# One decode-attention kernel on one core: values loaded two units at a time, keys of two units ahead of the values of both

## The chip, the cores and the metric

The kernel runs on one core of one Trainium2 chip. The metric is device time in microseconds (us) of one execution. The core has a matrix engine (TensorE, PE in the profile, with its weight loads shown apart as PEld), a vector engine (VectorE, DVE), a scalar engine (ScalarE, ACT), a general engine (GpSimd, POOL) and a sync engine (SyncE, SP) that here does nothing but issue DMA transfers and wait. Data comes from the off-chip memory (HBM) through 16 DMA engines into SBUF; TensorE writes to PSUM, and VectorE and ScalarE copy from there.

## The reference

One query token, 32 query heads, 8 key/value heads, 65,536 keys, head size 128, all bf16. Each key/value head serves R = 4 query heads.

```python
B, Hq, Hkv, Sq, Sk, D = 1, 32, 8, 1, 65536, 128
scale = D ** -0.5
scores = jnp.einsum("bhqd,bhkd->bhqk", q, k) * scale
p = _softmax(scores, axis=-1)
return jnp.einsum("bhqk,bhkd->bhqd", p, v)
```

Keys and values are 134.2 MB each, and each byte is used once, for four queries. Nothing of the result needs them twice.

## The kernel before

**Units.** A head's 65,536 keys are cut into HU = 4 units of 16,384 keys; with 8 heads there are NU = 32 units, numbered through. A unit of keys is one transfer of 4,096 KB: 128 partitions, each with a row of 32 KB that is contiguous in HBM (128 keys of 256 bytes). The same holds for a unit of values. There are two buffers for keys (`kbuf`) and two for values (`vbuf`); unit n uses number n % 2 of both.

**Keys of a unit** (`pe_keys`, L156). Keys lie with the key index on partitions, and a product over the head size needs them turned, so TensorE transposes them: 16 groups of TB = 8 transposes (L138) into one of four PSUM buffers (`trb`). Each group is copied to SBUF (`ktb`, `evict`, L220): groups 3, 7, 11 and 15 by ScalarE (L228), the other twelve by VectorE (L230). LAG = 3 groups later, eight matmuls (L149) with the copied keys as weights and the four queries as the moving operand write the scores (`qkb`, two buffers). A unit is done with its key buffer when its last group has been transposed, and `evict` then raises `kfree`.

**Softmax of a unit.** It is the running form: VectorE reduces the maximum per partition (L261), GpSimd takes it over all partitions (L384), VectorE makes the new maximum and its negative (L276 to L278), ScalarE makes the correction factor `alpha` and four exponentials with their sums (L350, L354) into `pts`. VectorE then rescales the running output `acc` and the running sum `lp` (L289 to L291).

**Values of a unit** (`pe_values`, L171). 128 matmuls (L168) add up the unit's output in PSUM. They wait for the load (`vrdy`) and for the exponentials (`exd`). VectorE adds the result to `acc` (`add_values`, L243) and raises `vfree`, which gives the value buffer back.

**Order on TensorE** (L211). A loop of 16 rounds, in each: keys of an even unit, values of the odd unit before it, keys of the odd unit, values of the even unit. So a unit's softmax runs while the next unit's keys are on TensorE. After the loop, `pe_last` (L178) does the values of unit 31.

**Order on VectorE and ScalarE.** VectorE's pass for unit u (`dve_pass`, L254) mixes the end of unit u with the evictions of unit u + 1: score maximum of u, output of u - 1, evictions 0 to 2 of u + 1, new maximum, six more evictions, sums and rescaling, the last three evictions. ScalarE does the same with its four evictions and the exponentials (`act_pass`, L344).

**Order of the loads.** SP issues all loads on one queue in the order K0, K1, V0, K2, V1, K3, V2, ..., K31, V30, V31. Each key load waits for `kfree` (L403), each value load for `vfree` (L413). The first and the last unit of keys come in two halves. The last unit of values comes in six pieces of 64, 32, 16, 10, 4 and 2 of the 128 rows' parts (`V_PIECES`), and `pe_last` waits for each piece, so that little is left to do when the last piece lands: 126 matmuls in the usual form, two in another form (L197), one that adds the running output (L201), a scaling (L339) and the store of the last head.

Of the kernel before, what the change touches and what calls it, by code (L numbers as in the profile page):

```python
# [5 lines left out]
DT = mybir.dt  # L6
# [4 lines left out]
P = 128  # L11
# [32 lines left out]
def bass_standalone__gqa_softmax__decode_kernel(nc, q, k, v, out):  # L44
# [6 lines left out]
    scale = float(D) ** -0.5  # L51
    kf, vf, qf, of = k[0], v[0], q[0, :, 0, :], out[0, :, 0, :]
# [28 lines left out]
    alpha = sb("alpha", [P, R], DT.float32)  # L81
# [19 lines left out]
    vrdy = [sem(f"vrdy{i}") for i in range(2)]  # L101
    vpiece = [sem(f"vpiece{i}") for i in range(len(V_PIECES))]
    kfree = [sem(f"kfree{i}") for i in range(2)]
    vfree = [sem(f"vfree{i}") for i in range(2)]
# [10 lines left out]
    def has_k(u):  # L115
        return u + 1 < NU

    def passes(e, one, start, period, last):

        for u in range(-1, start):  # L120
            one(u)
        n = (NU - 2 - start) // period
        with e.Fori(0, n):
            for u in range(start, start + period):
                one(u)
        for u in range(start + n * period, last + 1):
            one(u)
# [38 lines left out]
    def value(pe, b, t, first, last):  # L166
        vv = vbuf[b][:, :].rearrange("p (t d) -> p t d", d=D)
        return pe.matmul(pvb[b][:, 0:R], lhsT=vv[:, t, :], rhs=pts[b][:, t * R:(t + 1) * R],  # L168
                         start=t == first, stop=t == last)

    def pe_values(pe, b):  # L171
        take(pe, vrdy[b], 16)
        take(pe, exd)
        for t in range(T):
            ins = value(pe, b, t, 0, T - 1)
        ins.then_inc(pvd, 1)

    def pe_last(pe):  # L178
        b = (NU - 1) % 2
        vv = vbuf[b][:, :].rearrange("p (t d) -> p t d", d=D)  # L180
        starts = [sum(V_PIECES[:i]) for i in range(len(V_PIECES))]
        pe.wait_ge(t_o, 1)
        pe.transpose(qkb[0][0:HR - R, 0:P], oT[:, R:HR], identf[:, :]).then_inc(s_o, 1)
        take(pe, exd)
        for t in range(ROWS_FROM):
            if t == starts[1]:
                pe.wait_ge(t_lp, 1)
                pe.matmul(fin[0:R, P:P + 1], lhsT=lp[:, :], rhs=ones[:, :],
                          start=True, stop=True).then_inc(s_l, 1)
            if t == starts[-2]:  # L190
                pe.wait_ge(t_last, 1)
            ins = value(pe, b, t, 0, ROWS_FROM - 1)
            if t in starts:
                ins.wait_op(vpiece[starts.index(t)], 16, "sem-ge")
        ins.then_inc(pvd, 1)
        for t in range(ROWS_FROM, T):
            ins = pe.matmul(fin[0:R, 0:P], lhsT=pts[b][:, t * R:(t + 1) * R], rhs=vv[:, t, :],  # L197
                            start=t == ROWS_FROM, stop=False)
            if t in starts:
                ins.wait_op(vpiece[starts.index(t)], 16, "sem-ge")  # L200
        ins = pe.matmul(fin[0:R, 0:P], lhsT=acc[:, :], rhs=identf[:, :], start=False, stop=True)  # L201
        ins.wait_op(t_acc, 1, "sem-ge")
        ins.then_inc(s_fin, 1)

    def tensor_engine(pe):
        pe.wait_ge(q_sem, 16)
        pe.wait_ge(t_id, 1)
        pe.transpose(trb[0][:, 0:HR], qsb[:, :], ident[0:HR, 0:HR]).then_inc(s_x, 1)  # L208
        pe.wait_ge(t_qT, 1)
        pe.addr_align(256, offset=LOOP_SLOT, max_nops=16)  # L210
        with pe.Fori(0, NU // 2) as i:  # L211
            pe_keys(pe, 0)
            with pe.If(i > 0):
                pe_values(pe, 1)
            pe_keys(pe, 1)
            pe_values(pe, 0)
        pe_last(pe)
# [25 lines left out]
    def add_values(e, w):  # L243
        take(e, pvd)
        e.sem_inc(vfree[w % 2], 1)  # L245
        pv = pvb[w % 2][:, 0:R]
        if w % HU == 0:
            own(e, e.tensor_copy(acc[:, :], pv), xd)  # L248
        else:
            own(e, e.tensor_tensor(acc[:, :], acc[:, :], pv, ALU.add), xd)  # L250
        if w % HU == HU - 1:
            own(e, e.tensor_tensor(oT[:, HR - R:HR], acc[:, :], recip[:, :], ALU.mult), xd)

    def dve_pass(e, u):  # L254
        if u >= 0:
            take(e, qkd)
            if u % HU == HU - 1 and has_k(u):
                next_queries(e, qrdy)
            elif has_k(u):
                e.sem_inc(qrdy, 1)  # L260
            e.tensor_reduce(cmax[:, :], qkb[u % 2][:, :].rearrange("p (t g) -> p g t", g=R),  # L261
                            AX.X, ALU.max).then_inc(cm, 1)
        if u >= 1 and has_k(u):
            add_values(e, u - 1)
        part = [[j for j in range(a, b) if not on_act(j)] for a, b in ((0, 4), (4, 12), (12, G))]
        if has_k(u):
            for j in part[0]:
                evict(e, u + 1, j)
        if u >= 0:
            take(e, cma)  # L270
            mn, mo = m[u % 2], m[(u - 1) % 2]
            if u % HU == 0:
                e.tensor_copy(mn[:, :], cmaxa[:, :])
                e.tensor_scalar(negm[:, :], cmaxa[:, :], -scale, None, ALU.mult).then_inc(ng, 1)
            else:
                own(e, e.tensor_tensor(mn[:, :], mo[:, :], cmaxa[:, :], ALU.max), xd)  # L276
                e.tensor_tensor(dm[:, :], mo[:, :], mn[:, :], ALU.subtract)  # L277
                e.tensor_scalar(negm[:, :], mn[:, :], -scale, None, ALU.mult).then_inc(ng, 1)  # L278
        if has_k(u):
            for j in part[1]:  # L280
                evict(e, u + 1, j)
        if not has_k(u):
            add_values(e, u - 1)
        if u >= 0:
            take(e, sx)
            if u % HU == 0:
                own(e, e.tensor_copy(lp[:, :], rsum[:, :]), xd)
            else:
                own(e, e.tensor_tensor(acc[:, :], acc[:, :], alpha[:, :], ALU.mult), xd)  # L289
                own(e, e.tensor_tensor(lp[:, :], lp[:, :], alpha[:, :], ALU.mult), xd)  # L290
                own(e, e.tensor_tensor(lp[:, :], lp[:, :], rsum[:, :], ALU.add), xd)  # L291
            if u % HU == HU - 1 and has_k(u):
                e.sem_inc(lrd, 1)
        if has_k(u):
            for j in part[2]:
                evict(e, u + 1, j)
        if u >= 0 and u % HU == HU - 1 and has_k(u):
            take(e, lra)
            own(e, e.reciprocal(recip[:, :], la[:, :]), xd)
            own(e, e.tensor_copy(otmp[:, 0:HR - R], oT[:, R:HR]), xd)  # L300
            own(e, e.tensor_copy(oT[:, 0:HR - R], otmp[:, 0:HR - R]), xd)
# [15 lines left out]
    def vector_engine(e):  # L317
# [7 lines left out]
        passes(e, lambda u: dve_pass(e, u), 1, HU, NU - 4)  # L325
        e.sem_inc(t_o, 1)
        for u in range(NU - 3, NU):
            dve_pass(e, u)
# [15 lines left out]
    def act_pass(e, u):  # L344
        if has_k(u):
            evict(e, u + 1, 3)
        if u >= 0:
            take(e, ng)
            if u % HU:
                e.activation(alpha[:, :], dm[:, :], AF.Exp, scale=scale)  # L350
            sv = qkb[u % 2][:, :].rearrange("p (t g) -> p g t", g=R)
            pv = pts[u % 2][:, :].rearrange("p (t g) -> p g t", g=R)
            for g in range(R):
                ins = e.activation(pv[:, g, :], sv[:, g, :], AF.Exp, bias=negm[:, g:g + 1],  # L354
                                   scale=scale, accum_out=rsum[:, g:g + 1])
            own(e, ins, xa)
            e.sem_inc(exd, 1)
            e.sem_inc(sx, 1)
        if has_k(u):
            for j in (7, 11, 15):  # L360
                evict(e, u + 1, j)

    def scalar_engine(e):
# [3 lines left out]
        passes(e, lambda u: act_pass(e, u), 0, HU, NU - 1)  # L367
# [21 lines left out]
    def src(x, n):  # L389
        h, c = n // HU, n % HU  # L390
        return x[h, c * P * T:(c + 1) * P * T, :].rearrange("(p t) d -> p (t d)", p=P)

    def sync_engine(e):
# [16 lines left out]
        def load_v(n):  # L410
            b = n % 2
            if n >= 2:
                e.wait_ge(vfree[b], n // 2)  # L413
            if n == NU - 1:
                pieces(vbuf[b], src(vf, n), V_PIECES, vpiece)
            else:
                e.dma_start(vbuf[b][:, :], src(vf, n)).then_inc(vrdy[b], 16)
# [45 lines left out]
```

## Time and profile before

| What | Value |
|---|---|
| Median of 3 runs | 631.81 us (631.73 to 631.89) |
| The profiled execution's own time | 631.78 us |
| Its span, first to last instruction | 629.9 us |
| Bytes read from HBM | 268.44 MB |
| TensorE busy | 517.2 us, 82% |
| VectorE busy | 312.8 us, 50% |
| ScalarE busy | 182.4 us, 29% |
| Mean granted TensorE clock | 0.772 |

The span is the time between the first and the last instruction that the profile shows; 1.9 us of the execution lie outside of it. A row of a timeline has the start in us from the span's start, the length in us, the engine and line, the operation, what it writes and reads, how many instructions were merged, and in brackets how long the engine stood idle before and what ended that. "SPq" and the like are the engine's sequencer, which waits and issues. In a windows table each engine has its busy time and its number of instructions, followed by the granted TensorE clock (1.00 is full), the busy share of the DMA engines and the rate.

### The profile page before, as it was taken

The page shows a single profiled execution, that of the slowest core. Times are in us where ns is not written, and L with a number is a line of the kernel's source. Part 1 is how long each engine was busy: PE and PEld are TensorE (multiplying, and loading weights), DVE is VectorE, ACT ScalarE, POOL GpSimd, SP SyncE. Part 2 cuts the span into 40 slices and gives each one's busy share as a digit, 9 for nine tenths or more (in the row PEclk, how much of TensorE's full clock was granted, in tenths as well). Part 3 has the DMA queues.
Part 4 walks back from the last instruction along what each step waited for, and adds up shares of the span by engine and source line. Part 5 has one row for each costly group of instructions (what it writes and reads, how often), then busy time and mean ns, then how long its engine had stood idle before and what let it go on. Part 6 is the DMA issues. An engine that isn't in the chain of part 4 may idle for free. (4 is left out here: it accounts for less than half of the span.)

```text
span 629.9 us, 26837 instructions
## 1 busy us (share of the span) xinstructions
PE 517.2 (82%) x12294; PEld 509.2 (81%) x12294; DVE 312.8 (50%) x689; ACT 182.4 (29%) x410; POOL 15.9 (3%) x49
## 2 busy tenths in 40 slices
PE   4678987789788798877888788987879787798897
PEld 4678987789788788877888778987879787788896
DVE  5435654446544455534565344653446544455552
ACT  2213332133322233221332213332223322233231
POOL 0000000000000000000000000000000000000000
PEclk9788876788767787767877678876778776787776
DMA  8999999999999999999999999999999999999996
GB/s 366 431 430 433 431 433 433 431 433 433 431 433 433 433 433 431 431 429 431 431 433 433 433 433 433 431 429 433 431 429 431 431 433 433 433 433 433 421 442 285
DMA packets 10335, 268.61 MB, mean 426 GB/s; under 512 B 1235, under 2 KB 1491, under 8 KB 1747
## 3 DMA queue, kind: packets, MB, share of 16 engines
q1 hardware_dynamic: 10232, 268.44, 99.3%
q8 instruction: 7, 0.11, 0.1%
q14 instruction: 6, 0.04, 0.0%
q10 hardware_dynamic: 90, 0.02, 0.0%
HBM read 268.44 MB, written 0.01 MB: 426 GB/s over the span
## 5 line engine op out<-in xcount | busy, mean ns | idle before, releaser
L138 PE MATMUL trb<-ident,kbuf 128*128 128x128 bf16 x4096 | 354.7, 245 | 76.9 <-PEq L41 76.9
L138 PEld LDWEIGHTS trb<-ident,kbuf 128*128 128x128 bf16 x4096 | 287.9, 111 | 78.7 <-issue 78.6
L230 DVE COPY ktb<-trb 128x1024 bf16<-128x1024 bf16 x384 | 255.7, 690 | 157.4 <-PE trb L138 152.3
L228 ACT ACTIVATE ktb<-trb 128x1024 bf16<-128x1024 bf16 x128 | 131.0, 1023 | 435.2 <-PE trb L138 376.2
L149 PE MATMUL qkb<-qcur,ktb 128*128 128x4 bf16 x4096 | 172.5, 165 | 23.5 <-PEq L41 20.7
L149 PEld LDWEIGHTS qkb<-qcur,ktb 128*128 128x128 bf16 x4096 | 155.5, 97 | 27.0 <-issue 25.1
L168 PE MATMUL pvb<-pts,vbuf 128*128 128x4 bf16 x4094 | 112.3, 165 | 5.2 <-issue 2.0
L168 PEld LDWEIGHTS pvb<-pts,vbuf 128*128 128x128 bf16 x4094 | 110.2, 101 | 7.2 <-issue 4.6
L354 ACT ACTIVATE pts<-qkb,negm 128x128 bf16<-128x128 f32 x128 | 50.8, 551 | 0.0
L261 DVE TENSOR_REDUCE cmax<-qkb 128x4 f32<-128x512 f32 x32 | 22.1, 692 | 38.6 <-DVEq L41 37.6
L354 ACT ACTIVATION_READ_ACCUMULATOR pts<-qkb,negm 128x1 f32 x128 | 36.1, 282 | 0.0
L250 DVE TENSOR_TENSOR acc<-acc,pvb 128x4 f32<-128x4 f32 x23 | 3.6, 159 | 60.3 <-DVEq L41 60.3
L384 POOL PARTITION_ALL_REDUCE cmaxa<-cmax x32 | 11.8, 370 | 503.4 <-POOLq L41 503.4
L248 DVE COPY acc<-pvb 128x4 f32<-128x4 f32 x8 | 1.3, 161 | 24.2 <-DVEq L41 24.2
L239 DVE COPY qcur<-qT 128x4 bf16<-128x4 bf16 x8 | 1.4, 170 | 11.6 <-DVEq L41 11.5
L291 DVE TENSOR_TENSOR lp<-lp,rsum 128x4 f32<-128x4 f32 x24 | 3.9, 163 | 3.5
L277 DVE TENSOR_TENSOR dm<-m 128x4 f32<-128x4 f32 x24 | 3.9, 162 | 3.5
L290 DVE TENSOR_TENSOR lp<-lp,alpha 128x4 f32<-128x4 f32 x24 | 3.9, 162 | 3.5
L350 ACT ACTIVATE alpha<-dm 128x4 f32<-128x4 f32 x24 | 4.7, 198 | 2.7 <-ACTq L41 2.7
L387 POOL PARTITION_ALL_REDUCE la<-lp x7 | 3.0, 429 | 99.1 <-POOLq L41 99.1
L208 PE MATMUL trb<-ident,qsb 32*128 32x32 bf16 x1 | 0.2, 204 | 5.1 <-DMA qsb<-in_q_dram 5.1
L208 PEld LDWEIGHTS trb<-ident,qsb 32*128 32x128 bf16 x1 | 0.1, 100 | 5.1 <-DMA qsb<-in_q_dram 5.1
(43 smaller groups left out, 31.0 us busy)
## 6 DMA issues: line engine op xcount, KB each, us to landing
vbuf<-in_v_dram SPq DMA_DIRECT2D x31, 4096.0 KB, 31.4
kbuf<-in_k_dram SPq DMA_DIRECT2D x30, 4096.0 KB, 26.9
kbuf<-in_k_dram SPq DMA_DIRECT2D x4, 2048.0 KB, 16.7
vbuf<-in_v_dram SPq DMA_DIRECT2D x1, 2048.0 KB, 17.1
vbuf<-in_v_dram SPq DMA_DIRECT2D x1, 1024.0 KB, 19.3
vbuf<-in_v_dram SPq DMA_DIRECT2D x1, 512.0 KB, 20.1
vbuf<-in_v_dram SPq DMA_DIRECT2D x1, 320.0 KB, 20.4
vbuf<-in_v_dram SPq DMA_DIRECT2D x1, 128.0 KB, 20.2
```

What stands on the lines that cost most here:

```text
L138: ins = pe.transpose(trb[j % NTB][:, i * P:(i + 1) * P], kv[:, t, :], ident[:, :])
L149: ins = pe.matmul(qkb[b][:, t * R:(t + 1) * R], lhsT=ktb[:, off:off + P], rhs=qcur[:, :], start=True, stop=True)
L168: return pe.matmul(pvb[b][:, 0:R], lhsT=vv[:, t, :], rhs=pts[b][:, t * R:(t + 1) * R], start=t == first, stop=t == last)
L228: ins = e.activation(dst, trb[j % NTB][:, :], AF.Copy).then_inc(eva, 1)
L230: ins = e.tensor_copy(dst, trb[j % NTB][:, :]).then_inc(evd, 1)
L261: e.tensor_reduce(cmax[:, :], qkb[u % 2][:, :].rearrange("p (t g) -> p g t", g=R), AX.X, ALU.max).then_inc(cm, 1)
L277: e.tensor_tensor(dm[:, :], mo[:, :], mn[:, :], ALU.subtract)
L290: own(e, e.tensor_tensor(lp[:, :], lp[:, :], alpha[:, :], ALU.mult), xd)
L291: own(e, e.tensor_tensor(lp[:, :], lp[:, :], rsum[:, :], ALU.add), xd)
L350: e.activation(alpha[:, :], dm[:, :], AF.Exp, scale=scale)
L354: ins = e.activation(pv[:, g, :], sv[:, g, :], AF.Exp, bias=negm[:, g:g + 1], scale=scale, accum_out=rsum[:, g:g + 1])
L384: e.partition_all_reduce(cmaxa[:, :], cmax[:, :], P, bass.bass_isa.ReduceOp.max).then_inc(cma, 1)
```

## The change

Two things are put in pairs. The two value buffers become one of twice the size, which takes the values of two units in one load with rows of 64 KB; one semaphore `vrdy` tells of its landing and one `vfree` of its release, after the values of both units. And the work is ordered in rounds of two units a and b: TensorE does keys a, keys b, values a, values b.

So that the pair is contiguous in HBM, `src` cuts a head into two blocks of 32,768 keys, and each partition owns 64 KB of a block in place of 32 KB. A key load still brings 4,096 KB into one of two buffers: it takes the first or the second 32 KB of each partition's 64 KB. Which keys form a unit changes, the result does not. The queue's order becomes K0, K1, V0+1, K2, K3, V2+3, ..., K30, K31, V30, and the six pieces of V31; the value load of a round waits for `vfree` of the round before.

VectorE's and ScalarE's passes are written as rounds of two units with the same instructions. In VectorE's, the evictions of unit a stand alone, those of unit b are mixed with the softmax of a, and the softmax of b and the outputs of a and b follow them. `alpha` gets two buffers. The rescaling of `acc` moves to just ahead of the addition, and the last head's part of `oT` moves to `next_output`.

```diff
-    vbuf = [sb(f"vbuf{i}", [P, T * D], DT.bfloat16) for i in range(2)]
+    vbuf = sb("vbuf", [P, 2 * T * D], DT.bfloat16)
...
     def pe_values(pe, b):
-        take(pe, vrdy[b], 16)
+        if b == 0:
+            take(pe, vrdy, 16)
         take(pe, exd)
...
-        with pe.Fori(0, NU // 2) as i:
+        with pe.Fori(0, NR) as i:
             pe_keys(pe, 0)
-            with pe.If(i > 0):
-                pe_values(pe, 1)
             pe_keys(pe, 1)
             pe_values(pe, 0)
+            with pe.If(i < NR - 1):
+                pe_values(pe, 1)
         pe_last(pe)
...
+    def dve_round(e, i):
+        a, b = 2 * i, 2 * i + 1
+        evictions(e, a, PART)
+        scores_done(e, a)
+        evictions(e, b, PART[:1])
+        maximum(e, a)
+        evictions(e, b, PART[1:2])
+        add_sums(e, a)
+        evictions(e, b, PART[2:])
+        scores_done(e, b)
+        maximum(e, b)
+        add_sums(e, b)
+        rescale(e, a)
+        add_values(e, a)
+        rescale(e, b)
+        if i < NR - 1:
+            add_values(e, b)
+            e.sem_inc(vfree, 1)
+            if b % HU == HU - 1:
+                next_output(e)
...
+    def act_round(e, i):
+        a, b = 2 * i, 2 * i + 1
+        for j in (3, 7, 11, 15):
+            evict(e, a, j)
+        evict(e, b, 3)
+        exponentials(e, a)
+        for j in (7, 11, 15):
+            evict(e, b, j)
+        exponentials(e, b)
...
-    def src(x, n):
-        h, c = n // HU, n % HU
-        return x[h, c * P * T:(c + 1) * P * T, :].rearrange("(p t) d -> p (t d)", p=P)
+    def src(x, u, units=1):
+
+        h, c, half = u // HU, u % HU // 2, u % 2
+        rows = x[h, c * 2 * P * T:(c + 1) * 2 * P * T, :].rearrange("(p t) d -> p (t d)", p=P)
+        return rows[:, half * T * D:(half + units) * T * D]
...
-        load_k(0)
-        for n in range(NU - 1):
-            load_k(n + 1)
-            load_v(n)
-        load_v(NU - 1)
+        for i in range(NR):
+            load_k(2 * i)
+            load_k(2 * i + 1)
+            if i:
+                e.wait_ge(vfree, i)
+            if i < NR - 1:
+                e.dma_start(vbuf[:, :], src(vf, 2 * i, 2)).then_inc(vrdy, 16)
+        e.dma_start(vbuf[:, 0:T * D], src(vf, NU - 2)).then_inc(vrdy, 16)
+        pieces(vbuf[:, T * D:2 * T * D], src(vf, NU - 1), V_PIECES, vpiece)
```

NR is NU // 2 = 16 rounds. `scores_done`, `maximum`, `add_sums`, `rescale`, `add_values` and `exponentials` hold the instructions that `dve_pass` and `act_pass` had for one unit.

More of the change, by code (lines that the diff above doesn't have):

```diff
@@ L116, in has_k, with rounds @@
         return u + 1 < NU
[L118 to L127, printed above, removed]
+    def rounds(e, one):
+        with e.Fori(0, H - 1):
+            for i in range(HALVES):
+                one(i)
+        return range(NR - HALVES, NR)
     def pe_transposes(pe, b, j):
@@ L241, in next_queries, with evictions, scores_done, maximum @@
         own(e, e.tensor_copy(qT[:, 0:HR - R], qtmp[:, 0:HR - R]), xd)
-    def add_values(e, w):
+    PART = [[j for j in range(a, b) if not on_act(j)] for a, b in ((0, 4), (4, 12), (12, G))]
+    def evictions(e, n, parts):
+        for part in parts:
+            for j in part:
+                evict(e, n, j)
+    def scores_done(e, u):
+        take(e, qkd)
+        if u % HU == HU - 1 and has_k(u):
+            next_queries(e, qrdy)
+        elif has_k(u):
+            e.sem_inc(qrdy, 1)
+        e.tensor_reduce(cmax[:, :], qkb[u % 2][:, :].rearrange("p (t g) -> p g t", g=R),
+                        AX.X, ALU.max).then_inc(cm, 1)
+    def maximum(e, u):
+        take(e, cma)
+        mn, mo = m[u % 2], m[(u - 1) % 2]
+        if u % HU == 0:
+            e.tensor_copy(mn[:, :], cmaxa[:, :])
+            e.tensor_scalar(negm[:, :], cmaxa[:, :], -scale, None, ALU.mult).then_inc(ng, 1)
+        else:
+            own(e, e.tensor_tensor(mn[:, :], mo[:, :], cmaxa[:, :], ALU.max), xd)
+            e.tensor_tensor(dm[:, :], mo[:, :], mn[:, :], ALU.subtract)
+            e.tensor_scalar(negm[:, :], mn[:, :], -scale, None, ALU.mult).then_inc(ng, 1)
+    def add_sums(e, u):
+        take(e, sx)
+        if u % HU == 0:
+            own(e, e.tensor_copy(lp[:, :], rsum[:, :]), xd)
+        else:
+            own(e, e.tensor_tensor(lp[:, :], lp[:, :], alpha[u % 2][:, :], ALU.mult), xd)
+            own(e, e.tensor_tensor(lp[:, :], lp[:, :], rsum[:, :], ALU.add), xd)
+        if u % HU == HU - 1 and has_k(u):
+            e.sem_inc(lrd, 1)
+    def rescale(e, u):
+        if u % HU:
+            own(e, e.tensor_tensor(acc[:, :], acc[:, :], alpha[u % 2][:, :], ALU.mult), xd)
+    def add_values(e, u):
         take(e, pvd)
-        e.sem_inc(vfree[w % 2], 1)
-        pv = pvb[w % 2][:, 0:R]
-        if w % HU == 0:
+        pv = pvb[u % 2][:, 0:R]
+        if u % HU == 0:
             own(e, e.tensor_copy(acc[:, :], pv), xd)
@@ L250, in add_values @@
             own(e, e.tensor_tensor(acc[:, :], acc[:, :], pv, ALU.add), xd)
[L251 to L301, printed above, removed]
@@ L303, in identities, with next_output @@
+    def next_output(e):
+        take(e, lra)
+        own(e, e.reciprocal(recip[:, :], la[:, :]), xd)
+        own(e, e.tensor_copy(otmp[:, 0:HR - R], oT[:, R:HR]), xd)
+        own(e, e.tensor_copy(oT[:, 0:HR - R], otmp[:, 0:HR - R]), xd)
+        own(e, e.tensor_tensor(oT[:, HR - R:HR], acc[:, :], recip[:, :], ALU.mult), xd)
     def identities(e):
@@ L324, in vector_engine @@
         e.sem_inc(qrdy, 1)
-        passes(e, lambda u: dve_pass(e, u), 1, HU, NU - 4)
+        rest = rounds(e, lambda i: dve_round(e, i))
         e.sem_inc(t_o, 1)
-        for u in range(NU - 3, NU):
-            dve_pass(e, u)
+        for i in rest:
+            dve_round(e, i)
         e.sem_inc(t_lp, 1)
@@ L341, in vector_engine, with exponentials @@
         ins.then_inc(t_last, 1)
[L344 to L361, printed above, removed]
+    def exponentials(e, u):
+        take(e, ng)
+        if u % HU:
+            e.activation(alpha[u % 2][:, :], dm[:, :], AF.Exp, scale=scale)
+        sv = qkb[u % 2][:, :].rearrange("p (t g) -> p g t", g=R)
+        pv = pts[u % 2][:, :].rearrange("p (t g) -> p g t", g=R)
+        for g in range(R):
+            ins = e.activation(pv[:, g, :], sv[:, g, :], AF.Exp, bias=negm[:, g:g + 1],
+                               scale=scale, accum_out=rsum[:, g:g + 1])
+        own(e, ins, xa)
+        e.sem_inc(exd, 1)
+        e.sem_inc(sx, 1)
+    def act_round(e, i):
[7 more added lines that the diff above has]
+        exponentials(e, b)
     def scalar_engine(e):
@@ L366, in scalar_engine @@
         e.activation(dscr[:, 1:2], dscr[:, 0:1], AF.Exp, scale=1.0)
-        passes(e, lambda u: act_pass(e, u), 0, HU, NU - 1)
+        for i in rounds(e, lambda i: act_round(e, i)):
+            act_round(e, i)
         e.wait_ge(t_row, 1)
```

23 lines of the change are left out of this document (8 added, 15 removed).

## The prediction, made before the change was run

> **What bounds the kernel now.** I read the page first, for the engine that is never idle.
>
> ```profile
> span 629.9 us, 26837 instructions
> ...
> PE 517.2 (82%) x12294; PEld 509.2 (81%) x12294; DVE 312.8 (50%) x689; ACT 182.4 (29%) x410; POOL 15.9 (3%) x49
> ...
> DMA  8999999999999999999999999999999999999996
> GB/s 366 431 430 433 431 433 433 431 433 433 431 433 433 433 433 431 431 429 431 431 433 433 433 433 433 431 429 433 431 429 431 431 433 433 433 433 433 421 442 285
> ...
> q1 hardware_dynamic: 10232, 268.44, 99.3%
> ```
>
> The reader is to see that the DMA engines are busy in every slice but the first and the last, 99.3% of the span on the load queue, at one steady rate, while TensorE has 18% to spare. The loads bound the kernel. What can move the time is the rate of the loads, a hole in their queue, or what is left after the last load.
>
> Next the waits of SP and the page's list of issues, to see how full the queue stands.
>
> ```profile
> SPq L407 <- ACTq L226: 403.8, 29, 18.0
> SPq L417 <- DVEq L245: 142.5, 29, 7.0
> ```
>
> ```profile
> vbuf<-in_v_dram SPq DMA_DIRECT2D x31, 4096.0 KB, 31.4
> kbuf<-in_k_dram SPq DMA_DIRECT2D x30, 4096.0 KB, 26.9
> ```
>
> SP waits nearly always for a buffer, yet a load lands only 26.9 to 31.4 us after its issue. The timeline gives the time of one 4,096 KB load. TensorE starts on the keys of units 29, 30 and 31 here, the first two on their landing, and in 29 to 30 one load of keys and one of values pass.
>
> ```profile
> 568.47 3.57 PE L138 MATMUL trb<-ident,kbuf 128*128 128x128 bf16 x32 [2.35 <-PEq L41]
> 587.90 3.57 PE L138 MATMUL trb<-ident,kbuf 128*128 128x128 bf16 x32 [2.14 <-PEq L41]
> 600.60 0.34 PE L149 MATMUL qkb<-qcur,ktb 128*128 128x4 bf16 x8 [0.66 <-PEq L41]
> 601.05 3.52 PE L168 MATMUL pvb<-pts,vbuf 128*128 128x4 bf16 x128
> 604.43 3.57 PE L138 MATMUL trb<-ident,kbuf 128*128 128x128 bf16 x32
> 604.81 0.16 DVE L250 TENSOR_TENSOR acc<-acc,pvb 128x4 f32<-128x4 f32 x1 [2.93 <-DVEq L41]
> 608.87 0.61 PE L138 MATMUL trb<-ident,kbuf 128*128 128x128 bf16 x8
> 609.31 0.34 PE L149 MATMUL qkb<-qcur,ktb 128*128 128x4 bf16 x8
> 609.51 0.61 PE L138 MATMUL trb<-ident,kbuf 128*128 128x128 bf16 x8
> 617.30 0.34 PE L149 MATMUL qkb<-qcur,ktb 128*128 128x4 bf16 x8 [0.67 <-PEq L41]
> 617.63 3.49 PE L168 MATMUL pvb<-pts,vbuf 128*128 128x4 bf16 x128
> 617.79 0.69 DVE L261 TENSOR_REDUCE cmax<-qkb 128x4 f32<-128x512 f32 x1 [1.64 <-DVEq L41]
> 618.69 0.37 POOL L384 PARTITION_ALL_REDUCE cmaxa<-cmax  x1 [16.24 <-POOLq L41]
> 621.28 0.28 ACT L354 ACTIVATION_READ_ACCUMULATOR pts<-qkb,negm 128x1 f32 x1
> 621.93 1.87 PE L168 MATMUL pvb<-pts,vbuf 128*128 128x4 bf16 x64 [0.57 <-DMA vbuf<-in_v_dram]
> 626.51 0.56 PE L168 MATMUL pvb<-pts,vbuf 128*128 128x4 bf16 x14 [0.22 <-DMA vbuf<-in_v_dram]
> 627.00 0.37 PE L197 MATMUL pvb<-vbuf,pts 128*4 128x128 bf16 x2
> 627.94 0.34 DVE L339 TENSOR_SCALAR olast<-pvb,rl 4x128 bf16<-4x128 f32 x1 [0.68 <-PE pvb L201]
> ```
>
> 587.90 - 568.47 = 19.43 us for two loads, so one **slot** of 4,096 KB is 9.71 us. This stretch is also the kernel's end: the last scores are done at 617.30 + 0.34 = 617.64, the exponentials of unit 31 at 621.28 + 0.28 = 621.56, and from 621.93 on TensorE waits for each piece of the last values. The last load of values before the pieces, and nothing of TensorE, sets the time. The chain of waits agrees:
>
> ```profile
> 606.07 20.40 DMA vbuf<-in_v_dram
> 626.46 0.05 issue
> 626.51 0.56 PE pvb L168 x14
> ```
>
> So the last loads end at 626.46, and 627.07 - 626.46 = 0.6 us later the 126 matmuls are done.
>
> **The change, part by part.** First the steady rounds. Let L be the landing of a value pair. The next two key units land at L + 9.71 and L + 19.43, the next pair at L + 38.86 (four slots). TensorE does two units of values in 3.52 + 3.49 = 7.0 us, starts on keys a at about L + 10.3 (0.6 us behind a landing, as at the end above), and needs for one unit of keys:
>
> ```profile
> 296.47 3.57 PE L138 MATMUL trb<-ident,kbuf 128*128 128x128 bf16 x32 [2.75 <-PEq L41]
> 309.62 0.34 PE L149 MATMUL qkb<-qcur,ktb 128*128 128x4 bf16 x8 [0.66 <-PEq L41]
> 319.52 1.01 PE L138 MATMUL trb<-ident,kbuf 128*128 128x128 bf16 x8
> 320.59 1.01 PE L138 MATMUL trb<-ident,kbuf 128*128 128x128 bf16 x8
> ```
>
> That is 309.96 - 296.47 = 13.5 us here, 600.94 - 587.90 = 13.0 and 617.64 - 604.43 = 13.2 above; I take **13.2**. Every unit here starts slow and then speeds up, and the windows table shows why:
>
> ```profile
> 604.40:608.00 3.60, 3.60 (x45) 3.60 (x42) 2.30 (x5) 0.00 (x0) 0.00 (x0) 0.50 1.09 469
> 608.90:616.00 7.10, 7.10 (x182) 7.10 (x179) 6.06 (x12) 3.79 (x12) 0.00 (x0) 1.00 0.97 418
> ```
>
> The granted clock is 0.50 in the first microseconds after the values and a wait, and 1.00 after them. Keys b come straight behind keys a, which no row of before shows. If the clock stays up, their first four groups take 4 x (609.31 - 608.87) = 1.8 us in place of 3.57, so 13.2 - 1.8 = 11.4. If it falls in the pause at the end of keys a, they take up to 13.9 (13.5 and one more group at 320.59 - 319.52 = 1.07 in place of 609.51 - 608.87 = 0.64). I take **12.3**, nearer to the fast end, since TensorE comes from 8 us of full work. VectorE's score maximum of a (0.69) and ScalarE's exponentials now fall into keys b, as they fell into the next unit's keys before.
>
> The softmax of b used to run beside the next unit's keys. Now only values a cover it: last score to last sum is 621.56 - 617.64 = 3.9 us, and with the hand-over to TensorE (estimate) 4.1; values a take 3.5 of it where they are loaded. A round therefore needs 13.2 + 12.3 + 4.1 + 3.5 = 33.1 us of TensorE against 38.86 of loads. It fits with 5.8 us to spare.
>
> The queue: the next pair's load waits for the end of values b and an addition (604.81, 0.24 us behind 601.05 + 3.52), so it is issued at about L + 8. The two key loads ahead of it keep the engines busy until L + 19.4. Cover 11 us. Key loads of the next round are released at about L + 22 and L + 34, and are due at L + 38.9 and L + 48.6. Cover 14 us and more. So the moved waits (SP has in each of them only the loads behind it) and the single buffer cost nothing in the steady rounds; without these covers each microsecond would count 15 times.
>
> A page speaks against that: the Trainium skill, "Trainium Kernel Development and Optimization", Best Practices, asks for double buffering to overlap DMA with compute, and the values lose theirs. By it each round's load would stand still while values are used; by the rows above the key loads fill that time.
>
> The rate of the loads: half of the bytes now travel in rows of 64 KB in place of 32. No row of before has such a transfer. The nearest are 32 KB rows in the long stretch and the 16 KB rows of the last keys' halves:
>
> ```profile
> 50.00:596.00 546.00, 455.29 (x10844) 449.52 (x10842) 273.91 (x593) 160.85 (x368) 13.37 (x35) 0.77 1.00 432
> 597.00:606.00 9.00, 8.23 (x230) 8.07 (x228) 3.53 (x8) 1.74 (x2) 0.37 (x1) 0.76 1.02 433
> ```
>
> Per busy share that is 432 against 433/1.02 = 424.5, at most 1.8% from one doubling. What a fixed cost per row gives halves with each doubling, so 0.9% on half of 620 us of loads, **2.7 us of gain** at most. The two digits of the share make this a bound; I take a quarter, 0.7 us. As much may be lost instead (rows now start 64 KB apart), so -2.7 to +2.7.
>
> A rule speaks for the loss. The Trainium skill, "DMA: Bandwidth & Descriptors", Latency and other measured facts, gives less rate where partition rows lie at large powers of two apart, from 512 KB on; 64 KB is below that, and no row here shows a second pitch.
>
> **The end** is where the change costs. Counted back from the last landing at 626.46, the order is V31, V30, K31, K30 in place of V31, V30, K31, V29, K30. K31 still lands two slots before the end (607.0), but K30 lands one slot later, because V28 and V29 both travel ahead of it. TensorE starts on the keys of unit 30 at 587.90 + 9.71 - 0.7 = 596.9 and not at 587.90, and two units of keys must follow:
>
> - keys 30, 13.2 us: 610.1 (K31 has landed)
> - keys 31, 12.3 us: 622.4, against 617.64 before
> - softmax of unit 31, 4.1 us: 626.5; values 30 (3.5 us) run beside it
> - 126 of the 128 matmuls of unit 31 at full pace, 3.49 x 126/128 = 3.4 us: 629.9, against 627.07 before
>
> All pieces have landed by 626.5, so nothing there waits for data any more; the six pieces lose their use. From L197 on all is as before. The end moves by 629.9 - 627.07 = **+2.9 us**.
>
> One more cost can appear at that place. The first time TensorE ran values it stood still in the middle:
>
> ```profile
> 42.76 2.72 PE L168 MATMUL pvb<-pts,vbuf 128*128 128x4 bf16 x97 [2.04 <-issue]
> ```
>
> `pe_last` is code that runs once, and before it ran at the pace of the pieces. I take 0 and keep 0 to 2.0 us.
>
> The sum: the profiled execution took 631.78, 0.03 below the median of 631.81. 631.78 + 2.9 = **634.7 us**.
>
> **The rivals.**
>
> *The rows pay and the keys run fast (not slower).* 64 KB rows bring the full 2.7 us and the clock stays up through keys b. Keys 30 start at 587.90 + 9.71 - 2.7 = 594.9; + 13.0 + 11.4 + 4.1 + 3.4 = 626.8, against 627.07: 631.5 us. It decides from 2.9 us taken together out of the rows and the keys. For it: the engines are the bound all along. Against: the rate is one flat 431 to 433 already.
>
> *Rows of 64 KB are slower.* By the same 2.7 us the other way: keys 30 start 3.4 us later than forecast, 638.1. For it speaks only that the pitch is new.
>
> *TensorE becomes the bound of each round.* If the clock stayed at 0.50 over the keys, a unit would take 3.57 + 12 x 1.07 + 1.9 (the rest of a unit: 13.2 - 3.57 - 12 x 0.64) = 18.3, a round 36.6 + 7.6 = 44.2, 5.3 over the loads: 15 x 5.3 = 80, 712 us. Against: the clock always came up within 5 us, and rounds have longer unbroken work.
>
> *The single buffer opens a hole.* It decides when the pair's load is issued more than 19.4 us after the landing. Were values used with nothing queued, 7.0 + 1 us would be lost 14 times: 744 us. The two key loads ahead of it speak against.
>
> **How the numbers follow.** Forecast 0.80, rows paying 0.08, rows slower 0.08, TensorE as the bound 0.02, the hole 0.02. The forecast's own range: both keys 1 us faster or 3 slower (11.4 to 13.9 and 13.0 to 13.9), rows, and the code stop give 633 to 638. With the rival below I set **632.6 to 638.2**, which leaves out the two large cases and the fast half of the first rival. A measurement of this kernel can tell about 0.2% (1.3 us) from no change, so slower means over 633.1. Slower: 0.77 of the forecast's 0.80, and the three slow rivals, 0.89. Within: 0.03 and 0.05, 0.08. Faster: 0.03 of the first rival.
>
> **What would show it.** In the profile after: DMA 9 in all slices between the first and the last, and 431 to 434 GB/s; the first keys of unit 30 near 597; the last scores near 622.4; values of unit 31 in one run of 3.4 us with no wait for a load; the chain of waits with TensorE, VectorE and ScalarE at its end in place of the load of values. A granted clock of 0.50 inside keys b, or a stop by "issue" in the last values, would put the time higher. Wrong would be: a last piece that still lands after the exponentials of unit 31, a slice with a DMA digit under 9 in mid-run, or SP waiting on `vfree` while the queue is empty.

## The result and the profile after

| | before | changed |
|---|---|---|
| Median of 8 runs | 631.82 us (631.65 to 631.89) | 633.83 us (633.07 to 634.13) |
| Span of the profiled execution | 629.9 us | 632.0 us |
| TensorE busy | 517.2 us | 489.4 us |
| Mean granted TensorE clock | 0.772 | 0.789 |

The ratio is 1.0031 with a 95% interval of 1.0020 to 1.0041: the changed kernel is 2.0 us, or 0.3%, slower. 634.7 us was forecast, with a range of 632.6 to 638.2.

The page of the changed kernel answers to the first lines of before: the span, the DMA share and the rate by fortieths of the span, the load queue's share, and the issues of the value pairs with their time to landing.

```profile
span 632.0 us, 26791 instructions
...
DMA  8999999999999999999999999999999999999995
GB/s 367 450 418 444 428 425 442 433 446 419 431 448 415 448 415 431 448 415 448 415 431 452 413 450 417 450 428 417 450 423 456 415 431 452 417 450 412 417 431 203
...
q1 hardware_dynamic: 8072, 268.44, 98.7%
...
vbuf<-in_v_dram SPq DMA_DIRECT2D x15, 31.0
```

The digits stay at 9 between the first and the last slice: no round has a hole. The last digit fell from 6 to 5. The rate of a slice swings between 412 and 456 GB/s, where the prediction expected 431 to 434 in each; the mean from 50 to 596 us is 432 in both kernels. Why a slice swings stays open. A pair lands 31.0 us after its issue; two slots of 9.71 us are its own, so 11.6 us of other loads still stood ahead of it.

The chain of waits that ended last (start, length, what) shows the new end:

```profile
625.41 0.04 issue
625.46 1.85 PE pvb L166 x64
627.30 0.12 PE pvb L187 x2
627.43 1.75 PE pvb L166 x62
629.18 0.30 PE pvb L196 x2
...
630.05 0.34 DVE olast L357
```

Before, this chain held 20.40 us of a load, the fourth piece of the last values, and the last 14 matmuls started when it had landed. Now 64 and 62 matmuls run in one go with no load in the chain. The last scaling starts at 630.05 against 627.94 before: the 2.1 us are all there. The timeline of TensorE leads back from it, from the values of units 28 and 29 over the keys of units 30 and 31 to the values of unit 30:

```profile
586.98 6.97 PE L166 MATMUL pvb<-pts,vbuf 128*128 128x4 bf16 x256 [4.48 <-PEq L41]
596.50 3.57 PE L136 MATMUL trb<-ident,kbuf 128*128 128x128 bf16 x32 [2.56 <-PEq L41]
609.50 0.34 PE L147 MATMUL qkb<-qcur,ktb 128*128 128x4 bf16 x8 [0.69 <-PEq L41]
609.70 1.95 PE L136 MATMUL trb<-ident,kbuf 128*128 128x128 bf16 x32
620.94 0.34 PE L147 MATMUL qkb<-qcur,ktb 128*128 128x4 bf16 x8 [0.68 <-PEq L41]
...
629.11 0.37 PE L196 MATMUL pvb<-vbuf,pts 128*4 128x128 bf16 x2
```

TensorE has done the values at 593.95 and waits 2.56 us for the keys of unit 30. Keys 30 run from 596.50 to 609.84, keys 31 directly behind them to 621.28, and the two matmuls behind the 126 start at 629.11, against 627.00 before. The first 32 transposes take 3.57 us in the one and 1.95 us in the other. The windows table (busy time of each engine, then granted clock, DMA share, GB/s) has the reason:

```profile
596.50:600.50 4.00, 4.00 (x44) 4.00 (x45) 2.08 (x3) 0.39 (x1) 0.00 (x0) 0.50 1.01 430
601.00:609.00 8.00, 7.82 (x201) 7.70 (x197) 6.00 (x9) 2.85 (x4) 0.00 (x0) 1.00 1.05 451
610.00:620.00 10.00, 10.00 (x242) 9.82 (x240) 8.83 (x18) 4.99 (x13) 0.37 (x1) 1.00 0.93 397
```

Keys 30 start at half clock behind the values and the wait, keys 31 at full clock.

### The profile page after: what moved, and what is told of

Its sections match the earlier page's. It is cut to its first block, busy times and chain, and to the rows that moved or that the text cites. A ratio compares the mean times of both kernels' runs of the same rounds, so it can differ in the third digit from the quotient of the medians.

```text
span 632.0 us, 26791 instructions
## 1 busy us (share of the span) xinstructions
PE 489.4 (77%) x12294; PEld 482.3 (76%) x12294; DVE 312.0 (49%) x689; ACT 185.6 (29%) x410; POOL 15.9 (3%) x49
## 5 line engine op out<-in xcount | busy, mean ns | idle before, releaser
L136 PE MATMUL trb<-ident,kbuf 128*128 128x128 bf16 x4096 | 328.5, 233 | 41.3 <-PEq L41 41.3
L136 PEld LDWEIGHTS trb<-ident,kbuf 128*128 128x128 bf16 x4096 | 263.1, 105 | 42.3 <-issue 42.2
L147 PE MATMUL qkb<-qcur,ktb 128*128 128x4 bf16 x4096 | 170.7, 165 | 22.7 <-PEq L41 21.9
L147 PEld LDWEIGHTS qkb<-qcur,ktb 128*128 128x128 bf16 x4096 | 153.2, 97 | 26.7 <-issue 23.9
L369 ACT ACTIVATION_READ_ACCUMULATOR pts<-qkb,negm 128x1 f32 x128 | 34.6, 270 | 0.0
L407 POOL PARTITION_ALL_REDUCE cmaxa<-cmax x32 | 11.9, 371 | 580.6 <-POOLq L41 580.6
L266 DVE TENSOR_TENSOR m<-m,cmaxa 128x4 f32<-128x4 f32 x24 | 3.8, 159 | 11.5 <-DVEq L41 11.5
L238 DVE COPY qcur<-qT 128x4 bf16<-128x4 bf16 x8 | 1.4, 170 | 11.8 <-DVEq L41 11.6
L283 DVE TENSOR_TENSOR acc<-acc,alpha 128x4 f32<-128x4 f32 x24 | 3.9, 163 | 4.2 <-DVEq L41 1.7
```

The lines of the kernel that those rows point to most:

```text
L136: ins = pe.transpose(trb[j % NTB][:, i * P:(i + 1) * P], kv[:, t, :], ident[:, :])
L147: ins = pe.matmul(qkb[b][:, t * R:(t + 1) * R], lhsT=ktb[:, off:off + P], rhs=qcur[:, :], start=True, stop=True)
L283: own(e, e.tensor_tensor(acc[:, :], acc[:, :], alpha[u % 2][:, :], ALU.mult), xd)
L407: e.partition_all_reduce(cmaxa[:, :], cmax[:, :], P, bass.bass_isa.ReduceOp.max).then_inc(cma, 1)
```

## The experiments

Each run stands beside runs of the kernel before on the same chip; those had medians of 631.72 to 631.80 us. The first four take the sum apart: spacing of rows, length of rows, the wait for the keys of unit 30, and the pieces at the end.

**Only the spacing of the rows (x1_pitch).** The kernel before with

```diff
-    def src(x, n):
-        h, c = n // HU, n % HU
-        return x[h, c * P * T:(c + 1) * P * T, :].rearrange("(p t) d -> p (t d)", p=P)
+    def src(x, n):
+        h, c, half = n // HU, n % HU // 2, n % 2
+        rows = x[h, c * 2 * P * T:(c + 1) * 2 * P * T, :].rearrange("(p t) d -> p (t d)", p=P)
+        return rows[:, half * T * D:(half + 1) * T * D]
```

> The kernel before with nothing changed but which keys form a unit: each load's rows are still 32 KB, but start 64 KB apart, as the key loads of the changed kernel do. Theory (the spacing costs nothing, the 2.0 us come from the end): 631.8 us, within 0.3. Rival (the spacing slows the loads and longer rows of the values hide part of it): over 633 us, and the first transposes of unit 30 over 1 us later than 587.9.

Measured 631.84 us (11 runs), ratio 1.0000 (0.9991 to 1.0009). The keys of unit 30 start where they did:

```profile
587.98 3.57 PE L138 MATMUL trb<-ident,kbuf 128*128 128x128 bf16 x32 [2.90 <-PEq L41]
```

Rows that start 64 KB apart cost nothing that 11 runs could tell. The rival of slower rows falls.

**Only the length of the rows (x2_split).** The changed kernel with each pair loaded in two:

```diff
-            take(pe, vrdy, 16)
+            take(pe, vrdy, 32)
...
-                e.dma_start(vbuf[:, :], src(vf, 2 * i, 2)).then_inc(vrdy, 16)
+                e.dma_start(vbuf[:, 0:T * D], src(vf, 2 * i)).then_inc(vrdy, 16)
+                e.dma_start(vbuf[:, T * D:2 * T * D], src(vf, 2 * i + 1)).then_inc(vrdy, 16)
...
         e.dma_start(vbuf[:, 0:T * D], src(vf, NU - 2)).then_inc(vrdy, 16)
+        e.sem_inc(vrdy, 16)
```

> The changed kernel with each pair of values loaded by two loads with rows of 32 KB in place of one with rows of 64 KB. Theory (the long rows save about 1.1 us until the keys of unit 30, and the end follows those keys): first transposes of unit 30 at 597.6 in place of 596.5, time 634.9 us (634.2 to 635.5). Rival (the long rows bring nothing, the earlier keys are chance): 633.8 us, keys of unit 30 at 596.5.

Measured 635.04 us (634.35 to 635.67, 5 runs), ratio 1.0049 (1.0035 to 1.0063): 1.2 us above the changed kernel. Its timeline has keys 30 and the last values:

```profile
597.97 3.57 PE L136 MATMUL trb<-ident,kbuf 128*128 128x128 bf16 x32 [2.61 <-PEq L41]
610.74 0.34 PE L147 MATMUL qkb<-qcur,ktb 128*128 128x4 bf16 x8 [0.68 <-PEq L41]
626.71 1.85 PE L166 MATMUL pvb<-pts,vbuf 128*128 128x4 bf16 x64 [0.53 <-PEq L41]
```

Keys 30 start 1.47 us later than in the changed kernel and the last values 1.25 us later (keys 30 were quicker here by 13.34 - 13.11 = 0.2). The long rows do save time, and the end follows the start of keys 30. The DMA packets in the traces say where the saving is: a row of 64 KB took 2.423 us (mean of 1,920 packets), one of 32 KB 1.217 us (mean of 3,968). Two short rows cost 0.0114 us more than one long row (0.011 by the rounded figures); 8 such pairs per engine and load, 15 loads: 1.4 us. The split is not free of a second effect: 15 more loads bring 240 more packets of 4 bytes, at 0.009 us each 0.1 us per engine.

**The wait for the keys of unit 30 (x3_k30_halves).** The changed kernel with

```diff
-            if n in (0, NU - 1):
+            if n in (0, NU - 2, NU - 1):
```

> The changed kernel with the keys of unit 30 loaded in two halves, as those of units 0 and 31 are. Theory (the end waits for TensorE, which has two units of keys to do after the keys of unit 30 land): TensorE starts on them when it has done the values of unit 29, at about 593.9 in place of 596.5, and the end moves by the same 2.6 us, to 631.2 us (630.7 to 631.9). Rival (the loss lies in the rounds, not at the end): no gain, 633.5 us or more.

Measured 631.11 us (630.63 to 631.84, 11 runs), ratio 0.9988 (0.9979 to 0.9997). The timeline:

```profile
586.98 6.97 PE L166 MATMUL pvb<-pts,vbuf 128*128 128x4 bf16 x256 [4.92 <-PEq L41]
593.91 3.57 PE L136 MATMUL trb<-ident,kbuf 128*128 128x128 bf16 x32
607.46 0.34 PE L147 MATMUL qkb<-qcur,ktb 128*128 128x4 bf16 x8 [0.68 <-PEq L41]
618.89 0.34 PE L147 MATMUL qkb<-qcur,ktb 128*128 128x4 bf16 x8 [0.68 <-PEq L41]
623.41 1.84 PE L166 MATMUL pvb<-pts,vbuf 128*128 128x4 bf16 x64 [0.39 <-PEq L41]
```

The 2.56 us of waiting are gone, keys 30 start directly behind the values, and by the medians the end comes 2.7 us sooner. The profiled execution, the slowest of the eleven, gained 2.0 us, because its keys 30 took 607.80 - 593.91 = 13.89 us. Its first 32 transposes also take 3.57 us, with no wait between the values and the keys, so it isn't that wait that leaves the clock low. One condition in the order of loads wins back more than the whole change lost. The kernel is 0.7 us faster than before, small, but beyond the interval. It still ends on TensorE: the last values start at 623.41 and run without a wait for data.

**The pieces of the last values (x4_one_piece).** The changed kernel with

```diff
-        pieces(vbuf[:, T * D:2 * T * D], src(vf, NU - 1), V_PIECES, vpiece)
+        e.dma_start(vbuf[:, T * D:2 * T * D], src(vf, NU - 1)).then_inc(vpiece[0], 16)
+        for sm in vpiece[1:]:
+            e.sem_inc(sm, 16)
```

> The changed kernel with the values of unit 31 in one load in place of six. Theory (at the end TensorE waits for the softmax of unit 31 and no longer for data, so the pieces are of no use): 633.8 us, within 0.5. Rival (the pieces still shorten the end): later by up to the 3.4 us of the unit's matmuls, 635 to 637 us.

Measured 634.11 us (633.86 to 634.39, 5 runs), ratio 1.0035 (1.0021 to 1.0049). That is 0.3 us above the changed kernel's median, with the two ranges overlapping. The pieces are of no use there any more.

The next two measure the cover of the single value buffer, by giving it back later.

**Later by a little (y1_release_mid) and past the cover (y2_release_late).** In both, `e.sem_inc(vfree, 1)` is taken from behind the additions and SP waits for `i + 1`. The first raises it behind three evictions of the next a, the second behind its score maximum:

```diff
-        evictions(e, a, PART)
+        evictions(e, a, PART[:1])
+        e.sem_inc(vfree, 1)
+        evictions(e, a, PART[1:])
```

```diff
         scores_done(e, a)
+        e.sem_inc(vfree, 1)
         evictions(e, b, PART[:1])
```

> The changed kernel with the value buffer given back later: not behind the additions of values b but behind the first three evictions of the next unit a, at about 13.5 us after the pair's landing in place of 8. Theory (the two key loads ahead in the queue cover 19.4 us): 633.8 us, within 0.6. Rival (the single buffer has little to spare): each round longer by up to the 5.5 us of delay, 15 times, up to 716 us.

> The same with the buffer given back behind the score maximum of the next unit a, at about 24 us after the landing, past the cover of 19.4 us. Theory (the cover is used up there): a hole of 4.6 us in the load queue and about 2 us from issue to data, in 15 rounds, 5 to 6.6 us each: 709 to 733 us, with a DMA share under 0.9 in the middle of the run. Rival (the queue has more ahead than the two key loads, or the rounds are not bound by loads): under 640 us.

In the changed kernel a round in mid-run has these rows (the issue of a pair, the values of both its units, the issue of the next pair):

```profile
283.69 0.33 SPq L441 DMA_DIRECT2D vbuf<-in_v_dram  x1
315.01 6.97 PE L166 MATMUL pvb<-pts,vbuf 128*128 128x4 bf16 x256 [4.31 <-PEq L41]
322.47 0.33 SPq L441 DMA_DIRECT2D vbuf<-in_v_dram  x1
```

A pair lands 31.0 us after its issue, so this one landed at 314.7, and the next is issued 7.8 us behind that. In the first experiment the values start within 0.01 us of the same time and the issue stands at 327.40, 12.7 us behind the landing; it measured 634.27 us (633.79 to 634.81, 4 runs), ratio 1.0039 (1.0023 to 1.0054), no change that its spread could tell. In the second the values start at 315.18 and the next pair is issued at 337.76, 22.6 us later. The windows table shows a stretch just ahead of the pair's data, and then 280 us in mid-run:

```profile
334.40:338.60 4.20, 3.52 (x89) 3.43 (x87) 2.38 (x5) 1.02 (x1) 0.02 (x1) 1.00 0.00 0
300.00:580.00 280.00, 185.34 (x4696) 182.94 (x4693) 119.05 (x259) 72.08 (x163) 6.10 (x16) 0.75 0.87 371
```

For 4.2 us the DMA engines are idle. The run measured 730.35 us (729.43 to 732.39, 4 runs), ratio 1.1569: (730.35 - 633.83)/15 = 6.4 us per round. The hole that the rival feared exists and costs what was worked out, but only past the two key loads that stand ahead in the queue.

The last group tried to keep the long rows and give the end of before back, with the loads K28, K29, V28, K30, V29, K31, V30 and the values of unit 29 between keys 30 and keys 31.

**The order of before in the last two rounds (y3_before_tail).** SP's last rounds are written out in that order, V29 has a semaphore of its own, VectorE adds the values of unit 29 in the last round, and TensorE's loop gets a second copy of the values:

```diff
             pe_keys(pe, 0)
+            with pe.If(i > NR - 2):
+                pe_values(pe, 1, True)
             pe_keys(pe, 1)
             pe_values(pe, 0)
-            with pe.If(i < NR - 1):
+            with pe.If(i < NR - 2):
                 pe_values(pe, 1)
```

> The changed kernel with the order of before in the last two rounds alone: loads K28, K29, V28, K30, V29, K31, V30, V31 in pieces, and on TensorE keys 30, values 29, keys 31, values 30. Theory (long rows save 1.1 us in the rounds, and the end of before has no TensorE behind the loads): the last piece lands at about 625.4, the end is 1.1 us ahead of before, 630.7 us (630.3 to 631.2), faster than both kernels. Keys 31 again start at the low clock and need about 13.2 us in place of 11.6. Rival (the rounds lose something of their own that the end hides): over 631.8 us.

Measured 825.18 us (822.61 to 829.64, 5 runs), ratio 1.3052. The theory missed. The rival's bound, over 631.8 us, is met, but neither named what the run shows. Its page and its waits (who waited for what: total, times, longest) show a cost that goes through all rounds and not only the last two:

```profile
q8 instruction: 143, 2.34, 1.2%
```

```profile
PEld qkb L147 <- issue: 114.7, 71, 4.2
PE qkb L147 <- issue: 87.6, 38, 4.1
PE pvb L166 <- issue: 20.1, 16, 3.1
```

The kernels before and after have 7 packets on that instruction queue. Here it is 143, about 9 in each of the 16 rounds, and TensorE stands still in the middle of its work with nothing to wait for that the profile shows, while instruction packets come in.

**The same with the last rounds written out (z2_unrolled).** TensorE's loop runs over 14 rounds and has no copy more than the changed kernel's; behind it stand the two last rounds in the order of before.

```diff
-        with pe.Fori(0, NR) as i:
+        with pe.Fori(0, NR - 2):
             pe_keys(pe, 0)
             pe_keys(pe, 1)
             pe_values(pe, 0)
-            with pe.If(i < NR - 1):
-                pe_values(pe, 1)
+            pe_values(pe, 1)
+        pe_keys(pe, 0)
+        pe_keys(pe, 1)
+        pe_values(pe, 0)
+        pe_keys(pe, 0)
+        pe_values(pe, 1, True)
+        pe_keys(pe, 1)
+        pe_values(pe, 0)
```

> The order of before in the last two rounds once more, with TensorE's loop over the first 14 rounds and the last two written out behind it, so that the loop is no larger than in the changed kernel. Theory (long rows save 1.1 us, and the end of before has no TensorE behind the loads): last piece at 625.4, 630.7 us (630.3 to 631.4); keys 31 take about 13.2 us, starting at the low clock. Rival (code that runs once stalls TensorE at the end): 631.8 to 634 us, with idle time ended by issue in the last two rounds.

Measured 636.76 us (636.68 to 636.99, 5 runs), ratio 1.0079 (1.0065 to 1.0093): the theory missed, and the rival's stops are there, but the time lies above its 631.8 to 634 us. Of 18 instruction packets, 6 come in the first 55 us, none in the rest of the loop, and 12 from 562 us on, in the code behind the loop (keys 28 start at 557.2). In the timeline of the last two rounds

```profile
605.61 2.51 PE L136 MATMUL trb<-ident,kbuf 128*128 128x128 bf16 x22
610.11 1.25 PE L136 MATMUL trb<-ident,kbuf 128*128 128x128 bf16 x10 [2.00 <-issue]
...
628.80 1.39 PE L166 MATMUL pvb<-pts,vbuf 128*128 128x4 bf16 x47 [1.51 <-issue]
```

Keys 31 start at 605.61, 4.1 us sooner than in the changed kernel, but TensorE stops for 2.00 us within keys 31 and for 1.51 us within the last values, each time just behind the start of an instruction packet (at 607.53 and 626.46). Keys 31 also ran at a granted clock of 0.50 for 10 us (605.6 to 615.6) and took 622.51 - 605.61 = 16.9 us in place of the 13.2 expected; the stop of 2.00 us accounts for only a part of that. So the end of before on top of long rows was not measured free of this cost.

**Code that is never run (z1_dead_128, z3_dead_64, z5_dead_mid_128, z6_dead_mid_16).** The changed kernel with value matmuls behind a condition that never holds: 128 and 64 at the end of TensorE's loop, 128 and 16 between keys a and keys b.

```diff
+            with pe.If(i > NR):
+                for t in range(128):
+                    value(pe, 1, t, 0, 127)
```

> The changed kernel with 128 more value matmuls in TensorE's loop behind a condition that is never true: as much code as the second copy of the values had, with no change of any order. Theory (the 193 us of the kernel with the order of before in the last two rounds came from the size of TensorE's loop, whose code no longer stays on the core and is loaded anew each round): 780 to 830 us, some 140 instruction packets. Rival (they came from the order of the last loads or from waits): 633.8 us, 7 instruction packets on that queue.

> The same with 64 matmuls that are never run, half as much code. If the loop then still fits: 633.8 us and 7 instruction packets. If it does not: over 700 us. The theory doesn't say where the limit lies; the two runs bracket it.

> The changed kernel with the same 128 matmuls that are never run, now between keys a and keys b, where the kernel of 825 us has its second copy of the values; no order of loads or of executed work changes. Theory (the loop's code is loaded anew each round when a block that is skipped lies in its middle and makes it too long): 780 to 830 us and over 100 instruction packets. Rival (the 193 us came from the order of the last rounds): 634 us and 7 packets.

> The same place with 16 matmuls that are never run. If it is the length of the loop that counts: 634 us and 7 instruction packets. If it is the taken branch in the middle of the loop: over 700 us, as with 128.

Measured 634.27, 633.87, 633.75 and 633.99 us, each with 7 instruction packets; the 780 to 830 us of the two theories with 128 matmuls missed. But the four runs decide nothing on the size of the loop. In their traces TensorE executes 33 branches, as in the changed kernel, where the condition added in the 825 us kernel made it 49, one more in each of 16 rounds. So the condition was not in the program that ran, and these are runs of the changed kernel.

That the 825 us came with the loading of instructions in each round is shown by the packets and the stops. That one copy of the values too many made the loop too long for what the core keeps is argued only. An estimate from the packets of 16.4 KB (2.34 MB / 143): the changed kernel loads 6 of them, 98 KB, in its first 55 us and no more until 626.72, and the 825 us kernel 143/16 = 8.9, some 146 KB, in each round.

The four runs are of use for another question, the spread of the changed kernel's time (1.06 us over 8 runs, against 0.24 before). Here are the fastest and the slowest of the five profiles that the changed kernel now has, z5_dead_mid_128 and then z1_dead_128, from the start of keys 30 on:

```profile
596.41:599.41 3.00, 3.00 (x29) 3.00 (x30) 1.62 (x3) 0.00 (x0) 0.00 (x0) 0.50 0.99 421
599.45:603.00 3.55, 3.55 (x93) 3.55 (x90) 2.40 (x4) 1.62 (x2) 0.00 (x0) 1.00 1.00 425
```

```profile
596.64:602.48 5.84, 5.84 (x74) 5.84 (x75) 2.87 (x5) 1.02 (x1) 0.00 (x0) 0.50 0.99 424
602.52:606.00 3.48, 3.48 (x88) 3.48 (x86) 2.88 (x5) 1.02 (x1) 0.00 (x0) 1.00 1.09 466
```

| Profile | keys 30 start | clock at 1.00, behind that | keys 30 | span | span less keys 30 |
|---|---|---|---|---|---|
| z5_dead_mid_128 | 596.41 | 3.0 us | 12.8 us | 631.4 us | 618.6 us |
| z6_dead_mid_16 | 596.55 | 3.6 us | 13.0 us | 631.8 us | 618.8 us |
| changed | 596.50 | 4.3 us | 13.3 us | 632.0 us | 618.7 us |
| z3_dead_64 | 596.66 | 4.8 us | 13.5 us | 632.3 us | 618.8 us |
| z1_dead_128 | 596.64 | 5.9 us | 13.9 us | 632.7 us | 618.8 us |

The spans differ by 1.3 us and what is left without keys 30 by 0.2. The later the granted clock comes up within keys 30, the longer the run.

## Why the prediction was right

It held in direction, place and mechanism; two terms were too careful in size, and smaller misses the other way took back part of that.

| Step | forecast | measured |
|---|---|---|
| Steady rounds | no hole, 11 us of cover | DMA digit 9 between the first and the last slice, 11.6 us; a hole only when forced |
| Keys 30 start | 596.9 | 596.50 |
| Keys 30 | 13.2 us | 13.34 us |
| Keys 31 | 12.3 us (11.4 to 13.9) | 11.58 us |
| Softmax of unit 31 | 4.1 us | 625.46 - 621.28 = 4.18 us |
| Last values | 3.4 us, no wait for data | 629.18 - 625.46 = 3.72 us, no load in the chain |
| Stop for code in the last values | 0 (to 2.0) | none |
| End against before | +2.9 us | +2.1 us in the span, +2.0 us in the runs |

*The end.* The keys of unit 30 land one slot later because V29 now travels ahead of them (V28 did so before, too), and two units of keys, one softmax and one unit of values follow on TensorE. x3 shows the cause: only the landing of the first half of K30 was moved, and the end moved with it. x4 shows that the pieces of the last values no longer count there. The prediction reads the 20.40 us load in the chain of before as the last one ahead of the pieces; it is the fourth piece. The landing at 626.46 that it counts from is right all the same.

*Keys 31.* This term was taken 0.7 us too long. The clock stayed at 1.00 through the pause of 0.69 us between the units, so the fast bound of 11.4 us was nearly right. The rounds in mid-run agree: keys b took 11.4 to 11.9 us in all 15 rounds behind the first, keys a 12.8 to 14.0. The prediction also says that the clock always came up within 5 us; in the trace of before that took 2.7 to 6.0 us from a unit's first transpose.

*The long rows.* 0.7 us of gain was taken, a quarter of a bound of 2.7, and no row of before showed which part to take: the sign was argued, the size guessed. x2 measured 1.2 to 1.5 us and the packets give 1.4. In the sum it appears as keys 30 starting 597.61 - 596.50 = 1.1 us ahead of the slot count.

*The last values* are 0.3 us longer than the pace of the matmuls; the sum of `lp` (0.12 us in the chain) stands between them.

*Added up.* Keys 30 start 0.4 us sooner, keys 31 are 0.72 us shorter, and they start 0.14 us ahead of the last scores of keys 30: 1.26 us less. Keys 30, the softmax and the last values are 0.14, 0.08 and 0.32 us longer: 0.54 us more. That is the 0.72 us between the 629.9 forecast for the end of the 126 matmuls and 629.18. Without the second group the miss would have been 1.3 us. Part of the closeness is luck: keys 30 can take anything from 12.8 to 13.9 us, and 13.2 lies in the middle of that.

*The rivals.* Slower rows fell with x1. TensorE as the bound of a round did not come: in mid-run a round's values begin at 315.01, 0.3 us behind the landing of the pair. Of the rival that was not slower, half came: keys 31 ran fast, but the rows brought 1.1 to 1.5 us and not 2.7. The hole needed a release past the two key loads, as y2 shows.

*The spread.* The changed kernel's runs spread over 1.06 us, those of before over 0.24. Before, the end was set by the loads; now it follows keys 30, which start at the low clock, and the five profiles above show that their length is what the span varies with. What decides how soon the clock comes up stays open.

## What to carry to other kernels

When a stream of loads bounds a kernel, count back from the last byte: the work that depends on the last few loads is the only compute that shows, and grouping loads moves that work toward the end even where each round has room to spare. A single buffer in place of two costs nothing as long as other loads stand in the queue for longer than the buffer takes to come free; the issue-to-landing time in the page, less the load's own time, is that cover. Where the end has become compute, look for the last load that compute waits for and split that one: splitting the keys of unit 30 won 2.7 us here, while the pieces of the last values, which come behind it, were of no use any more.

## What the runs showed of the hardware that was not expected

- TensorE's loop with one more copy of the values (128 matmuls, behind a condition) went from 7 instruction packets to 143 and from 633.8 to 825.2 us.
- Code written out behind the loop was loaded as it was reached, and TensorE stopped for 2.00 and 1.51 us beside these loads (z2). In the changed kernel a packet came at 626.72, within its last values, and no such stop appeared.
- In the trace of the changed kernel the granted clock is 0.50 or 1.00, and it kept one value for 3.41, 10.24, 13.65, 17.07, 20.48 or 23.89 us at a time, up to the last stretch: multiples of 3.41. In the 6.97 us of 256 value matmuls at 315.01 it stayed at 0.50, with TensorE busy all the time.
- A row of 64 KB took 2.423 us where two of 32 KB took 2 x 1.217 = 2.434 us, so 0.011 us is saved by each joining, and starting rows 64 KB apart in place of 32 cost nothing that 11 runs could tell.
